# Attention and expert layer on one core: squares of the weights on ScalarE, two more weight pieces in the first loads, a third place for x, scales and splits earlier

## The chip, the core and the metric

The kernel runs on one core of a Trainium2 chip. The metric is the device time of one execution in microseconds (us), lower is better. A core has TensorE (PE, with its weight loads shown as PEld), VectorE (DVE), ScalarE (ACT), GpSimd (POOL) and SyncE (SP), whose queue issues every DMA of this kernel. Each engine works through its own list of instructions in the order of the built program, and waits on semaphores for the others.

## What is computed

The reference is a linear attention, whose output is the input of a feed-forward layer with a gate:

```python
q_s = np.exp(q - q.max(-1, keepdims=True));  q_s /= q_s.sum(-1, keepdims=True) + 1e-09
k_s = np.exp(k - k.max(2, keepdims=True));   k_s /= k_s.sum(2, keepdims=True) + 1e-09
kv = np.einsum('bhsd,bhse->bhde', k_s, v)            # batch 8, heads 8, seq 576, head_dim 64
x = np.einsum('bhsd,bhde->bhse', q_s, kv)            # then transposed to 4608 tokens x 512
h = x @ w_in                                          # 512 x 2048
g = h * erf(softplus(h))
out = g @ w_out                                       # 2048 x 512
```

All inputs are float32 here, except that the two weight matrices arrive as 64-bit numbers, which the kernel reads as pairs of 32-bit integers and turns into float32 itself.

## The kernel before

**Tiling.** The 4608 tokens are 12 blocks of 384 (`T`), three blocks for two batches. The 2048 columns of the hidden layer are four quarters. An item `n` is one block and one quarter, so there are 48; items 0 to 3 are block 0, items 4 to 7 block 1 and so on. An item has these steps, whose letters stand in the string `ORDER`: `m` is x times w_in (into `pX`, `pY`, `pZ`, from there to `H`), `T` softplus and `G` erf on ACT, `U` the product with h on DVE (L931), `I` and `O` the high and the low half of the result in float16 (L946 and L950), and `M` the product with w_out (into `o`).

**Two kinds of items.** Items 0 to 3 multiply in float32: `mm1_32` (L894) and the branch of `mm2` at L969. They need the weights only as float32. From item 4 on both products run in float16 with a high and a low half of each operand: seven products for four quarters of the matrices at L855, and three matmuls for one at L978. For them the weights are scaled and split (`wsplit`, `wsplit_sums`, letters `S` and `R`), and so is x (`finish`, steps `f`).

**Weights.** There are eight jobs, a quarter of w_in or of w_out each, in the order of `JOBS` (jobs 0, 1, 3 and 5 are w_in's, 2, 4, 6 and 7 w_out's), and each is loaded in two pieces of 1 MB (`wload`). A piece lands in one of several places (`raw`, or the tiles `wt` of jobs whose split is still far off); `wdecode` (letter `D`, L190, L194, L197) turns it into float32 with three DVE operations and, as it frees the place, asks for the next piece. `LOADS` is the order of the first loads: each `w` in it is one piece.

**Scales.** `wsquares` (`Q`) finds a bound of the squares of a job: 16 matmuls of 128x128 blocks with themselves (L224, tile `gram`) and a maximum on DVE (L225). `wscales` (`Z`, from L236) needs all eight, and gives the scales; no split can be done ahead of it.

**Attention.** The generator `attention(b)` hands out batch b in small shares; each `A` in `ORDER` takes one, and from item 4 on `pace` takes as many as a goal says, worked out from `n1`, `SHARES` and `LEAD`. Its matmuls for k and v are `kv_mm` (L503, tiles `kv_0` and `kv_1`), after which the loads of the next batch's k and v are issued (`load_kv`). x of a batch is written from PSUM by ACT (`x_put`, L405), times a scale `sx` for batches 0 and 1. `x_free` says when a block of x has a place; there are two.

**What sets the order.** The code is emitted as `ORDER` says, and then item by item; a scheduler of the framework then orders the instructions of each engine by what they depend on. `SPLITS` names the splits that are emitted in items 4 to 6. SP issues its DMAs in the order of its list: one that must wait holds up all that stand behind it.

Of the kernel before, what the change touches and what calls it, by code (L numbers as in the profile page):

```python
# [9 lines left out]
F32 = mybir.dt.float32  # L10
I32 = mybir.dt.int32
BF16 = mybir.dt.bfloat16
AF = mybir.ActivationFunctionType
# [9 lines left out]

CHAIN_FROM, CHAIN_TAIL = 2, 11

LOADS = "qkwwvwww"

# [4 lines left out]
    qm0 qm1 kmax kT kB qe0 qn0 ks2 ks0 D0.0 ks1 ke2 ke0 ke1 w6 kv0 kn0 D0.1 qe1 qn1 kv1 t0  # L34
    kn1 kvs x0 t1 lkv t2 x2 t3 x1 x3
    m0.0 D1.0 m0.1 D1.1 m0.2 m0.3 T0 G0 Q0
    D2.0 A m1.0 D2.1 m1.1 U0 m1.2 m1.3 T1 G1 Q1 A A D3.0 M0.0 D3.1 M0.1 M0.2 Q2 U1 A
    m2.0 D4.0 m2.1 D4.1 m2.2 m2.3 T2 G2 Q3 A A M1.0 D5.0 M1.1 D5.1 M1.2 U2 A A Q4
    m3.0 D6.0 m3.1 D6.1 m3.2 m3.3 T3 G3 A A A M2.0 D7.0 M2.1 D7.1 M2.2 U3 Q5 Q6 Q7 Z A A A A
    S0 R0 f0 f1 M3.0 M3.1 M3.2 S1 R1  # L40
"""

SPLITS = {4: "S2 S3 R3", 5: "S4 S5 R5", 6: "S6 S7"}

SHARES = [2.51, 0, 0.16, 0.09, 1.58, 2.43, 1.12, 0.26, 0.29, 0.04, 0.78, 1.12, 0.16]
LEAD = 2.0
# [7 lines left out]
def attn_moe_kernel(  # L54
# [158 lines left out]

    def wsquares(jn):

        which, g = wjobs[jn]
        o = 24 + 4 * (which == "out") + g
        bk = bank(f"gram_{jn}")  # L220
        top = stg[jn].bitcast(BF16).rearrange("p (n two) -> p n two", two=2)[:, :, 1]
        for i in range(16):
            blk = top[:, i * P:(i + 1) * P]
            nc.tensor.matmul(bk[:, :P], blk, blk, start=(i == 0), stop=(i == 15))  # L224
        nc.vector.tensor_reduce(small[:, o:o + 1], bk[:, :P], axis=AX.X, op=ALU.max)  # L225
        wsq.add(jn)

    def wscales():
# [99 lines left out]
    def x_free(i):  # L328


        return i < 2 or (("m", NG - 1, 3) in emitted if i == 2 else i - 2 in x7)

    def xblock(i):

        if i not in xbl:
            assert x_free(i)
            xbl[i] = xp.tile([P, NC4, T], F32, tag="xs", name=f"x_{i}")
        return xbl[i]

    x_next = [1]  # L340
# [60 lines left out]
    def bank(name):  # L401
        return psa.tile([P, 512], F32, tag="bk", name=name)
# [191 lines left out]
    def x_split(b, c, bk):  # L594
        for blk, off, o, w in xcols(b, 0 if b % 2 == 0 else SM + 2 * TAIL, SM):
            x_put(
                bk[:, o:o + w], xblock(blk)[:, c, off:off + w],
                bat[b]["sx"] if b < E32 else None,
            )

    def attention(b):
# [298 lines left out]
    def unit(b, g):  # L900

        U = bat[b]["U"][:, g:g + 1]
        if b < 2 and (b, g) not in udone:
            udone.add((b, g))
            nc.vector.tensor_tensor(U, w_u["in"][:, g:g + 1], bat[b]["ux"], op=ALU.mult)
        return U
# [3 lines left out]
    def flat(t):  # L910
        return t.rearrange("p f t -> p (f t)")
# [4 lines left out]
    def softplus(n):  # L916
        s, g = st[n], seq[n][2]
        s["G"] = ch.tile([P, FG, T], F32, tag="G", bufs=2, name=f"G_{n}")
        for o, w, b in spans(n):
            h, sp = s["H"], s["G"]  # L920
            h, sp = (flat(t) if w == T else t[:, :, o:o + w] for t in (h, sp))
            u = bat[0]["ux"] if n < NG else unit(b, g)
            act(sp, h, AF.Softplus, chain=in_chain(n), scale=u)

    def erf(n):
# [2 lines left out]

    def gmul(n):
        s, g = st[n], seq[n][2]  # L930
        nc.vector.scalar_tensor_tensor(  # L931
            flat(s["G"]), flat(s["G"]), bat[0]["ux"] if n < NG else GA[:, g:g + 1],
            flat(s["H"]), op0=ALU.mult, op1=ALU.mult,
        )
        if n < NG:
            return
        assert "all" in wready

        hl = flat(s["H"]).bitcast(F16)
        s["gh"], s["gl"] = (  # L940
            hl[:, i * GE:(i + 1) * GE].rearrange("p (f t) -> p f t", f=FG) for i in range(2)
        )
# [113 lines left out]
    w_even = sum(SHARES[:9]) + NC4 * sum(SHARES[11:])  # L1056
    w_odd = w_even + sum(SHARES[9:11])
    per_pair = w_even + w_odd
    n1 = NG + 1

    def pace(at_n):

# [67 lines left out]
```

## Time and profile before

| | us |
|---|---|
| median of 3 runs | 897.55 (896.29 to 899.88) |
| profiled execution, its time | 895.81 |
| its span, first to last instruction | 894.0 |
| PE busy | 841.5 (94% of the span) |
| DVE busy | 659.0 (74%) |
| ACT busy | 484.8 (54%) |

Busy time is the time in which at least one instruction of an engine ran; matmuls overlap, so their durations add up to more. The profiled execution took 895.81, of which 1.8 us lie outside the span. A line of the timeline shows the start, how long it took, the engine, the line of the kernel and the tiles; in brackets stands how long the engine had been idle and what ended that.

### The profile page before, as it was taken

What the parts mean: (1) busy time and instruction counts of PE and PEld (TensorE: products, weight loads), DVE (VectorE), ACT (ScalarE), POOL (GpSimd) and SP (SyncE); (2) the same over time, 40 slices, a digit from 0 to 9 for tenths busy, and PEclk for the clock granted to TensorE, in tenths of its full rate; (3) what the DMA queues carried; (4) which work ended last, traced back from release to release, by engine and by line L of the source; (5) the groups of instructions that cost most, each with busy time, mean ns of one, the idle gap of its engine ahead of it and who ended that gap; (6) DMA issues with size and microseconds to landing.
All of it is one profiled execution on the core that took longest, in us unless ns stands there. A gap on an engine that the chain in (4) does not pass through costs nothing.

```text
span 894.0 us, 15683 instructions
## 1 busy us (share of the span) xinstructions
PE 841.5 (94%) x6684; PEld 581.4 (65%) x6684; DVE 659.0 (74%) x908; ACT 484.8 (54%) x581; POOL 6.4 (1%) x14
## 2 busy tenths in 40 slices
PE   2899997688989999999999999999999999999997
PEld 1555554665766766766767767767767767676763
DVE  7889669999996687876896596877885575644453
ACT  2274156775673655654663655644754645553532
POOL 2000000000000000000000000000000000000000
PEclk9999998799999999999999999999999999999999
DMA  9864812401124120412033120311010000000100
GB/s 272 297 201 153 226 40 71 101 1 24 25 60 99 26 60 1 92 46 48 1 83 78 25 60 12 84 50 35 14 48 1 11 26 2 24 14 1 36 1 35
DMA packets 117381, 55.53 MB, mean 62 GB/s; under 512 B 106560, under 2 KB 108608, under 8 KB 117312
## 3 DMA queue, kind: packets, MB, share of 16 engines
q1 hardware_dynamic: 117312, 54.54, 22.2%
q8 instruction: 52, 0.85, 0.4%
q14 instruction: 17, 0.14, 0.0%
HBM read 45.09 MB, written 9.44 MB: 61 GB/s over the span
## 4 chain that ended last, share of the span: by engine, by line
PE 66%; DVE 21%; ACT 10%; issue 2%; DMA 1%; SPq 0%; ACTq 0%; DVEq 0%
PE o L978 27%; PE pX L855 14%; PE pZ L855 7%; ACT G L317 5%; ACT L317 4%; PE o L969 3%; PE pY L855 3%; DVE G L931 3%; DVE H L950 3%; PE kv L503 2%; PE pX L894 2%; DVE kmax L459 2%; DVE H L946 1%; DVE wt L270 1%; PE pY L894 1%
## 5 line engine op out<-in xcount | busy, mean ns | idle before, releaser
L978 PE MATMUL o<-wt,H 128*128 128x512 f16 x1584 | 366.7, 379 | 4.5 <-DVE H L950 3.2
L855 PEld LDWEIGHTS <-wt 128*128 128x128 f16 x3696 | 312.6, 99 | 47.8 <-issue 23.3
L978 PEld LDWEIGHTS <-H 128*128 128x128 f16 x1584 | 152.4, 98 | 158.8 <-DVE H L950 3.8
L855 PE MATMUL pX<-x,wt 128*128 128x192 f16 x2112 | 206.9, 248 | 6.5 <-DVE H L877 4.6
L317 ACT ACT_TABLE_LOAD x104 | 133.4, 1283 | 8.9 <-DVE H L880 7.1
L931 DVE SCALAR_TENSOR_TENSOR G<-G,small,H 128x1536 f32<-128x1536 f32 x44 | 80.0, 1817 | 69.0 <-ACT G L317 68.7
L855 PE MATMUL pZ<-x,wt 128*128 128x192 f16 x1056 | 104.6, 248 | 6.5 <-ACT x L269 4.7
L882 ACT COPY H<-pX 128x384 f32<-128x384 f32 x44 | 21.0, 477 | 148.8 <-PE pX L855 148.8
L317 ACT ACTIVATE G<-H,U 128x768 f32<-128x768 f32 (+1 forms) x60 | 72.8, 1231 | 22.1 <-DVE H L880 21.5
L950 DVE TENSOR_TENSOR H<-G,H 128x1536 f16<-128x1536 f32 x44 | 77.3, 1756 | 1.0
L317 ACT ACTIVATE G<-G 128x1536 f32<-128x1536 f32 x48 | 71.2, 1484 | 0.5
L855 PE MATMUL pY<-x,wt 128*128 128x192 f16 x528 | 52.3, 248 | 4.6 <-DVE H L867 4.6
L405 ACT ACTIVATE x<-x 128x384 f32<-128x384 f32 (+1 forms) x48 | 15.9, 378 | 56.5 <-PE x L590 54.8
L867 DVE COPY H<-pY 128x384 f32<-128x384 f32 x44 | 24.3, 552 | 30.0 <-PE pY L855 30.0
L946 DVE CAST H<-G 128x1536 f16<-128x1536 f32 x44 | 42.0, 956 | 0.8
L994 DVE TENSOR_SCALAR ob<-o,V 128x512 f32<-128x512 f32 x29 | 21.7, 747 | 25.4 <-PE o L978 25.3
L270 DVE SCALAR_TENSOR_TENSOR x<-x,x 128x768 f16<-128x768 f32 (+1 forms) x44 | 37.2, 848 | 4.2 <-ACT x L269 4.1
L269 ACT ACTIVATE x<-x 128x768 f16<-128x768 f32 (+1 forms) x44 | 33.0, 761 | 12.7 <-DVE x L361 12.7
L880 DVE TENSOR_TENSOR H<-pZ,H 128x384 f32<-128x384 f32 x44 | 24.2, 550 | 19.0 <-PE pZ L855 19.0
L869 DVE TENSOR_TENSOR H<-pX,H 128x384 f32<-128x384 f32 x44 | 24.3, 553 | 14.7 <-PE pX L855 14.5
L361 DVE TENSOR_TENSOR x<-x 128x384 f32<-128x384 f32 x44 | 24.2, 551 | 7.0 <-ACT x L405 6.7
L877 DVE TENSOR_TENSOR H<-pX,H 128x384 f32<-128x384 f32 x44 | 24.2, 549 | 5.1 <-PE pX L855 5.0
(158 smaller groups left out, 811.8 us busy)
## 6 DMA issues: line engine op xcount, KB each, us to landing
out_dram<-ob SPq DMA_DIRECT2D x32, 256.0 KB, 2.3
vbuf<-in_v_dram SPq DMA_DIRECT2D x60, 128.0 KB, 3.1
wt<-in_moe_w_out_dram SPq DMA_DIRECT2D x7, 1024.0 KB, 8.7
q<-in_q_dram SPq DMA_DIRECT2D x56, 128.0 KB, 2.9
k<-in_k_dram SPq DMA_DIRECT2D x56, 128.0 KB, 3.1
wt<-in_moe_w_in_dram SPq DMA_DIRECT2D x5, 1024.0 KB, 8.9
raw<-in_moe_w_in_dram SPq DMA_DIRECT2D x3, 1024.0 KB, 6.8
H_raw<-in_k_dram SPq DMA_DIRECT2D x2, 512.0 KB, 6.6
```

Source lines behind the costliest of these rows:

```text
L269: nc.scalar.activation(hi, src, AF.Copy, scale=s)
L270: nc.vector.scalar_tensor_tensor(lo, src, s, hi, op0=ALU.mult, op1=ALU.subtract)
L317: i = nc.scalar.activation(out_, in_, func, **kw)
L855: nc.tensor.matmul(o, w[wl][:, c, a * P:(a + 1) * P], x[:, xl, xi, c, :], start=(new and a == 0 and c == 0 and i == 0), stop=(c == 1 and i ...
L867: nc.vector.tensor_copy(C[0, 0], bank2("Y"))
L869: add(C[0, 0], bank2("X"), C[0, 0], op=ALU.add)
L894: nc.tensor.matmul(ph[:, :T], w[:, c, a * P:(a + 1) * P], x[:, c, :], start=(c == 0), stop=(c == NC4 - 1),)
L931: nc.vector.scalar_tensor_tensor(flat(s["G"]), flat(s["G"]), bat[0]["ux"] if n < NG else GA[:, g:g + 1], flat(s["H"]), op0=ALU.mult, op1=A ...
L946: nc.vector.tensor_copy(flat(s["gh"]), flat(s["G"]))
L950: nc.vector.tensor_tensor(flat(s["gl"]), flat(s["G"]), flat(s["gh"]), op=ALU.subtract)
L969: nc.tensor.matmul(o, s["G"][:, a, ts_], w[:, a, :], start=(first_ and a == 0), stop=(last_ and a == FG - 1),)
L978: nc.tensor.matmul(o, s[gt][:, a, ts_], w[wl][:, a, :], start=(first_ and a == 0 and i == 0), stop=(last_ and a == FG - 1 and i == 2),)
```

## The change

- `wsquares` leaves the matmuls away: four ACT operations `Square` over 128x512 each, with a sum along the row (`accum_out`), and a maximum of the four sums on DVE. PE has no part in it any more. What ACT writes besides the sums goes to a PSUM bank and is not read.
- `LOADS` has two more `w`: the first loads are seven pieces and not five. The two pieces that used to be asked for by the first two decodes are now issued at the start; the first two decodes ask for the next two.
- x has three places (`bufs=3`), and `x_free` follows.
- Block 0's x is stored without a scale; softplus of items 0 to 3 has a scale of 1, and their product `U` is a plain product of two tensors.
- In `ORDER` some decodes and shares of the attention are moved; `Z`, `S0` and `R0` stand ahead of `M2` now and not behind it, `S1`, `R1` ahead of `M3` and `S2` right behind it. `SPLITS` has the rest, earlier by one or two. `n1` is larger by two, which lets `pace` begin later and then go faster.

```diff
-LOADS = "qkwwvwww"
+LOADS = "qkwwvwwwww"
...
-    D2.0 A m1.0 D2.1 m1.1 U0 m1.2 m1.3 T1 G1 Q1 A A D3.0 M0.0 D3.1 M0.1 M0.2 Q2 U1 A
-    m2.0 D4.0 m2.1 D4.1 m2.2 m2.3 T2 G2 Q3 A A M1.0 D5.0 M1.1 D5.1 M1.2 U2 A A Q4
-    m3.0 D6.0 m3.1 D6.1 m3.2 m3.3 T3 G3 A A A M2.0 D7.0 M2.1 D7.1 M2.2 U3 Q5 Q6 Q7 Z A A A A
-    S0 R0 f0 f1 M3.0 M3.1 M3.2 S1 R1
+    D2.0 A m1.0 D2.1 m1.1 U0 m1.2 m1.3 T1 G1 Q1 A A D3.0 M0.0 D3.1 M0.1 M0.2 Q2 U1 A A
+    m2.0 D4.0 m2.1 D4.1 m2.2 m2.3 T2 G2 Q3 A A D5.0 M1.0 D5.1 M1.1 M1.2 U2 A A Q4 D6.0
+    m3.0 D6.1 m3.1 D7.0 m3.2 D7.1 m3.3 T3 G3 Q5 Q6 Q7 Z A A S0 A A R0 M2.0 A A M2.1 A A M2.2
+    A A f0 f1 U3 S1 R1 M3.0 M3.1 M3.2 S2
...
-SPLITS = {4: "S2 S3 R3", 5: "S4 S5 R5", 6: "S6 S7"}
+SPLITS = {4: "S3 R3 S4", 5: "S5 R5 S6", 6: "S7"}
...
-        bk = bank(f"gram_{jn}")
-        top = stg[jn].bitcast(BF16).rearrange("p (n two) -> p n two", two=2)[:, :, 1]
-        for i in range(16):
-            blk = top[:, i * P:(i + 1) * P]
-            nc.tensor.matmul(bk[:, :P], blk, blk, start=(i == 0), stop=(i == 15))
-        nc.vector.tensor_reduce(small[:, o:o + 1], bk[:, :P], axis=AX.X, op=ALU.max)
+        m = at.tile([P, 4], F32, tag="sq", name=f"sq_{jn}")
+        for i in range(4):
+            nc.scalar.activation(
+                bank(f"sq_{jn}_{i}"), stg[jn][:, i * 512:(i + 1) * 512], AF.Square,
+                accum_out=m[:, i:i + 1],
+            )
+        nc.vector.tensor_reduce(small[:, o:o + 1], m, axis=AX.X, op=ALU.max)
...
-        return i < 2 or (("m", NG - 1, 3) in emitted if i == 2 else i - 2 in x7)
+        return i < 3 or (("m", NG - 1, 3) in emitted if i == 3 else i - 3 in x7)
...
-            xbl[i] = xp.tile([P, NC4, T], F32, tag="xs", name=f"x_{i}")
+            xbl[i] = xp.tile([P, NC4, T], F32, tag="xs", bufs=3, name=f"x_{i}")
...
-                bat[b]["sx"] if b < E32 else None,
+                1.0 if blk == 0 else bat[b]["sx"] if b < E32 else None,
...
-            u = bat[0]["ux"] if n < NG else unit(b, g)
+            u = 1.0 if n < NG else unit(b, g)
...
+        if n < NG:
+            nc.vector.tensor_tensor(flat(s["G"]), flat(s["G"]), flat(s["H"]), op=ALU.mult)
+            return
...
-    n1 = NG + 1
+    n1 = NG + 3
```

Three places of the built program show how instructions move. The first is PE, item 1's product with w_out (`o_0`, `o_1`, `o_2`) and around it; `kv_0` and `kv_1` are the matmuls of k and v of batch 1, and `pX_0` begins item 3. Before:

```order
L969 MATMUL o_0_468<-wt_99,G_426 128x512 x4
L969 MATMUL o_1_478<-wt_99,G_426 128x512 x4
L969 MATMUL o_2_483<-wt_99,G_426 128x512 x4
L503 MATMUL kv_1_630<-vbuf,k_1_291 64x65 x8
L503 MATMUL kv_1_630<-vtail,kt_109 64x65 x2
L503 MATMUL kv_1_630<-vbuf,k_1_291 64x65 x8
L503 MATMUL kv_1_630<-vtail,kt_109 64x65 x2
L894 MATMUL pX_0_708<-x_134,wt_100 128x384 x4
```

After:

```order
L969 MATMUL o_0_452<-wt_99,G_418 128x512 x4
L969 MATMUL o_1_462<-wt_99,G_418 128x512 x3
L502 MATMUL kv_1_576<-vbuf,k_1_294 64x65
L969 MATMUL o_1_462<-wt_99,G_418 128x512
L502 MATMUL kv_1_576<-vbuf,k_1_294 64x65 x7
L502 MATMUL kv_1_576<-vtail,kt_109 64x65 x2
L502 MATMUL kv_1_576<-vbuf,k_1_294 64x65
L969 MATMUL o_2_467<-wt_99,G_418 128x512
L502 MATMUL kv_1_576<-vbuf,k_1_294 64x65 x7
L502 MATMUL kv_1_576<-vtail,kt_109 64x65 x2
L969 MATMUL o_2_467<-wt_99,G_418 128x512 x3
L893 MATMUL pX_0_683<-x_136,wt_100 128x384 x3
```

The matmuls of `kv_1` end with three of the four products of `o_2` still to come, where all twelve stood ahead of them before.

The second is SP's list. `raw`, `wt_93` and `wt_94` are the three places through which the last weight pieces come, `k_0`, `k_1`, `kt`, `vbuf` and `vtail` the loads of k and v (the first `vbuf` for batch 1, the others for batch 2); the load of `k_1` waits until the matmuls of `kv_1` have read the batch before. Before:

```order
L174 DMA wt_94<-in_moe_w_out_dram 128x2x1024
L381 DMA vbuf<-in_v_dram 128x4x64 x4
L174 DMA raw_615<-in_moe_w_out_dram 128x2x1024
L174 DMA wt_93<-in_moe_w_out_dram 128x2x1024
L381 DMA k_0_656<-in_k_dram 128x4x64 x4
L381 DMA k_1_661<-in_k_dram 128x4x64 x4
L395 DMA kt_666<-in_k_dram 64x8x64 x2
L381 DMA vbuf<-in_v_dram 128x4x64 x4
L395 DMA vtail<-in_v_dram 64x8x64
L174 DMA wt_94<-in_moe_w_out_dram 128x2x1024
```

After:

```order
L174 DMA wt_94<-in_moe_w_out_dram 128x2x1024
L380 DMA vbuf<-in_v_dram 128x4x64 x4
L380 DMA k_0_602<-in_k_dram 128x4x64 x4
L380 DMA k_1_607<-in_k_dram 128x4x64 x4
L394 DMA kt_612<-in_k_dram 64x8x64 x2
L380 DMA vbuf<-in_v_dram 128x4x64 x4
L394 DMA vtail<-in_v_dram 64x8x64
L174 DMA raw_626<-in_moe_w_out_dram 128x2x1024
L174 DMA wt_93<-in_moe_w_out_dram 128x2x1024
L174 DMA wt_94<-in_moe_w_out_dram 128x2x1024
```

The second piece of job 6 (`raw`) and the first of job 7 (`wt_93`) stood ahead of the loads of k and now stand behind them; the last piece (`wt_94`) is where it was.

The third is DVE between the last pieces and the scales. `sg_714` and `sg_778` (after: `sg_677` and `sg_698`) are the float32 weights of jobs 6 and 7, `wse_in` the first operation of the scales behind the transposes on PE. Before:

```order
L225 TENSOR_REDUCE small<-gram_689 128x1
L190 TENSOR_SCALAR sg_778<-wt_94 128x1024
L194 SCALAR_TENSOR_TENSOR sg_778<-wt_94,sg_778 128x1024
L197 SCALAR_TENSOR_TENSOR sg_778<-wt_94,sg_778 128x1024
L931 SCALAR_TENSOR_TENSOR G_740<-G_740,x_u,H_707 128x1536
L270 SCALAR_TENSOR_TENSOR x_1_947<-x_135,x_1_947 128x768
L416 TENSOR_REDUCE qt_m<-qt_760 128x8
L417 TENSOR_TENSOR qt_760<-qt_760,qt_m 128x512
L225 TENSOR_REDUCE small<-gram_794 128x1
L225 TENSOR_REDUCE small<-gram_812 128x1
L225 TENSOR_REDUCE small<-gram_830 128x1
L240 TENSOR_REDUCE wse_in<-ws_in 128x4
```

After:

```order
L194 SCALAR_TENSOR_TENSOR sg_677<-raw_626,sg_677 128x1024
L197 SCALAR_TENSOR_TENSOR sg_677<-raw_626,sg_677 128x1024
L190 TENSOR_SCALAR sg_698<-wt_93 128x1024
L931 TENSOR_TENSOR G_717<-G_717,H_682 128x1536
L194 SCALAR_TENSOR_TENSOR sg_698<-wt_93,sg_698 128x1024
L190 TENSOR_SCALAR sg_698<-wt_94 128x1024
L197 SCALAR_TENSOR_TENSOR sg_698<-wt_93,sg_698 128x1024
L194 SCALAR_TENSOR_TENSOR sg_698<-wt_94,sg_698 128x1024
L224 TENSOR_REDUCE small<-sq_730 128x1
L197 SCALAR_TENSOR_TENSOR sg_698<-wt_94,sg_698 128x1024
L224 TENSOR_REDUCE small<-sq_740 128x1
L239 TENSOR_REDUCE wse_in<-ws_in 128x4
```

Between the last decode (its third row is the last L197) and `wse_in` now stands one small maximum; item 3's product (L931), one row of x's split, two on the next batch's `qt` and three maxima stood there before. Three decodes stand in a row now, the first of them begun one row ahead of these, and item 3's product is among them.

## Rows read from the trace of the kernel before

**Rows 1.** The profile's page: span, and busy time of each engine.

```profile
span 894.0 us, 15683 instructions
PE 841.5 (94%) x6684; PEld 581.4 (65%) x6684; DVE 659.0 (74%) x908; ACT 484.8 (54%) x581; POOL 6.4 (1%) x14
```

**Rows 2.** Busy time of each engine by stretch; the first row names columns.

```profile
core 0: us, PE busy (x) PEld busy (x) DVE busy (x) ACT busy (x) POOL busy (x), PEclk, DMA share, GB/s
39.40:126.93 87.53, 86.55 (x425) 50.05 (x424) 70.89 (x91) 40.74 (x47) 0.95 (x1) 1.00 0.57 167
...
142.50:222.15 79.65, 61.07 (x520) 46.07 (x519) 74.94 (x101) 52.12 (x61) 0.00 (x0) 0.87 0.17 41
222.15:328.60 106.45, 102.99 (x897) 73.65 (x896) 86.47 (x120) 59.61 (x76) 0.00 (x0) 1.00 0.23 56
328.60:894.00 565.40, 554.99 (x4655) 390.24 (x4652) 379.82 (x509) 308.66 (x362) 0.00 (x0) 1.00 0.13 33
```

**Rows 3.** Groups by line: PE's matmuls for the squares (busy, mean ns).

```profile
L224 PE MATMUL gram<-wt 128*128 128x128 bf16 x96 | 6.5, 218 | 0.0
L224 PE MATMUL gram<-sg 128*128 128x128 bf16 x32 | 2.0, 218 | 0.0
```

**Rows 4.** Timeline of DVE from the last piece to the scales, and later.

```profile
113.30 0.69 DVE L190 TENSOR_SCALAR sg<-wt 128x1024 int32<-128x1024 int32 x1 [7.61 <-DMA wt<-in_moe_w_out_dram]
115.29 1.24 DVE L197 SCALAR_TENSOR_TENSOR sg<-wt,sg 128x1024 int32<-128x1024 int32 x1
117.88 1.82 DVE L931 SCALAR_TENSOR_TENSOR G<-G,x_u,H 128x1536 f32<-128x1536 f32 x1 [1.36 <-ACT G L317]
...
124.66 0.29 DVE L225 TENSOR_REDUCE small<-gram 128x1 f32<-128x128 f32 x1 [2.70 <-PE gram L224]
...
126.93 0.69 DVE L240 TENSOR_REDUCE wse_in<-ws_in 128x4 f32<-128x512 f32 x1
...
152.14 0.54 DVE L867 COPY H<-pY 128x384 f32<-128x384 f32 x1
```

**Rows 5.** Timeline of SP's queue: loads of batch 2's k, and the last piece.

```profile
90.64 11.61 SPq L381 DMA_DIRECT2D k<-in_k_dram  x8
...
107.14 1.51 SPq L174 DMA_DIRECT2D wt<-in_moe_w_out_dram  x1
```

**Rows 6.** Timeline of PE: item 1's product, `kv_1`, first float16 product, items 6 and 12.

```profile
87.20 10.57 PE L969 MATMUL o<-wt,G 128*128 128x512 f32 x24
...
99.19 0.33 PE L503 MATMUL kv<-vtail,kt 64*64 64x65 f32 x4
...
142.92 1.15 PE L855 MATMUL pY<-x,wt 128*128 128x192 f16 x12
...
221.42 0.81 PE L978 MATMUL o<-wt,H 128*128 128x512 f16 x3
...
328.60 1.67 PE L978 MATMUL o<-wt,H 128*128 128x512 f16 x7
```

**Rows 7.** Groups of ACT, shapes apart: rows of 512 and of 1536 elements.

```profile
L317 ACT ACTIVATE G<-G 128x1536 f32<-128x1536 f32 x48 | 71.2, 1484 | 0.5
...
L317 ACT ACTIVATE qt<-qt 128x512 f32<-128x512 f32 x4 | 2.5, 617 | 3.3 <-DVE qt L417 3.3
```

**Rows 8.** Groups of DVE: operations of the attention and of x's split.

```profile
L270 DVE SCALAR_TENSOR_TENSOR x<-x,x 128x768 f16<-128x768 f32 (+1 forms) x44 | 37.2, 848 | 4.2 <-ACT x L269 4.1
L429 DVE TENSOR_TENSOR q<-q,q_r 128x1024 f32<-128x1024 f32 x16 | 19.5, 1218 | 0.1
L572 DVE TENSOR_TENSOR qTs<-qT,qTs 128x512 f16<-128x512 f32 x24 | 16.4, 684 | 6.0 <-ACT qTs L571 6.0
L557 DVE SCALAR_TENSOR_TENSOR kvbd<-kvf,x_s,kvbd 64x256 f16<-64x256 f32 x12 | 5.8, 480 | 0.3
L556 DVE TENSOR_SCALAR kvbd<-kvf,x_s 64x256 f16<-64x256 f32 x12 | 4.2, 347 | 0.2
```

**Rows 9.** Group of PE: the attention's products that make x.

```profile
L590 PE MATMUL x<-qTs,kvbd 128*128 128x512 f16 x72 | 20.7, 379 | 2.9 <-DVE kvbd L556 1.6 <-ACT qTs L571 0.7 <-DVE qTs L572 0.5
```

More of the change, by code (lines that the diff above doesn't have):

```diff
@@ L930, in gmul @@
         s, g = st[n], seq[n][2]
+        if n < NG:
+            nc.vector.tensor_tensor(flat(s["G"]), flat(s["G"]), flat(s["H"]), op=ALU.mult)
+            return
         nc.vector.scalar_tensor_tensor(
-            flat(s["G"]), flat(s["G"]), bat[0]["ux"] if n < NG else GA[:, g:g + 1],
-            flat(s["H"]), op0=ALU.mult, op1=ALU.mult,
-        )
-        if n < NG:
-            return
+            flat(s["G"]), flat(s["G"]), GA[:, g:g + 1], flat(s["H"]),
+            op0=ALU.mult, op1=ALU.mult,
+        )
         assert "all" in wready
```

## The prediction

> **What bounds the kernel now.** The page comes first: PE is busy for 841.5 of 894.0 us and DVE for 659.0 [rows 1]. That is an average over stages with different limits, so the table by stretches comes next [rows 2]. In the float32 stage (39.4 to 126.93) PE is full, 86.55 of 87.53, and DVE is not, 70.89. From 142.5 to 222.15 it is the other way round: DVE works 74.94 of 79.65 us and PE 61.07, at a granted clock of 0.87. From 222.15 on PE is nearly full again: 102.99 of 106.45, then 554.99 of 565.4. So there are three limits in turn: PE, then DVE, then PE. What the middle one is worth shows in the lag: PE ends item 4's first float16 product at 144.1 [rows 6], and DVE copies it at 152.14 [rows 4], 8.1 us later. DVE is late because it idled before: 16.6 us in the float32 stage [rows 2], of which 7.61 in one wait for the last weight piece, and 2.70 in one wait for the matmuls of the squares [rows 4]. All scales begin at 126.93 [rows 4]; no split comes before. So I ask three things: when the scales begin, how much DVE has to do from there to item 6, and what PE has left from there.
>
> **Squares on ACT.** PE loses 128 matmuls. Their mean of 218 ns would make 27.9 us, but they overlap: the busy time of the two groups is 6.5 + 2.0 = 8.5 us, 1.06 a job [rows 3]. ACT gets 32 operations of 512 elements, at the row of ACT of that width 0.62 each [rows 7], so 20 us; beside ACT's 40.74 of 87.53 in the float32 stage [rows 2] there is room. No row shows one with a sum along the row: the lower bound is 0.62, the upper 1.48, ACT's row of three times the width; I take 0.62, whose width it is. On the path stand the last two squares of the last job, 1.2 us (up to 3.0), and five squares that the order of the change puts ahead of batch 1's exponentials of k, which have slack, since PE comes to `kv_0` only after item 2's products.
>
> **The last pieces and the scales.** In SP's list the last three pieces stand behind the loads of batch 2's k, which wait for `kv_1`. Before, `kv_1` ended at 99.5 [rows 6]. Four groups of matmuls for squares ahead of it go, 4.2 us [rows 3], and it moves ahead of three of item 1's twelve products: 10.57 / 12 x 3 = 2.6 us [rows 6]. That makes 92.7. SP took from 99.5 to 107.14 for the loads in between, 7.6 us [rows 5, 6], and the piece was there at 113.30, 6.2 us after its issue [rows 4]: the first of the three is now there at 92.7 + 7.6 + 6.2 = 106.5. DVE decodes three pieces in a row, each 0.69 + 1.24 + 1.24 (the middle operation taken like the last) = 3.2 [rows 4], together 9.5, and item 3's product among them, 1.8 [rows 4]: 117.8. The other two pieces are issued right behind and land while the first is decoded; if each needed its own 6.2 us, the end would be at 92.7 + 7.6 + 18.6 + 3.2 = 122.1. Behind the last decode come two squares and a transpose on PE, for which I take 2.0: the scales begin at 119.8 and not at 126.93. **That is -7.1**; with dearer squares, later pieces and PE's queue between 0 and -10. The two more pieces at the start cost nothing on the path: SP issues them while it would wait for PE's transposes, and the loads of batch 1 that land later by them are hidden by the decodes that they make possible, which DVE now does first; without that cover they would cost up to 2 x 6.2 us. Their gain, decodes without a wait, is in the sum above: DVE comes to the last three pieces early, and must wait there for the same loads that held up one piece before. So most of DVE's idle time stays, and that is why the gain is not 16.6.
>
> **DVE from the scales to item 6.** The instructions of DVE between `wse_in` and item 6's low half are the same, except that attention of batch 2 has moved behind: one operation like L429, two like L572, two like L557, two like L556, so 1.2 + 1.4 + 1.0 + 0.7 = 4.3 us [rows 8], and some tiny ones that I leave out. One of x's split has come in, 0.8 [rows 8]. **That is -3.5.** DVE's idle time in this stretch, 79.65 - 74.94 = 4.7 [rows 2], I leave as it is; it may vanish (-4.7) or double. The unscaled x of block 0 saves next to nothing: ACT stores the rest of the same product with the scale a few rows further, and waits there for the same scale; the plain products of items 0 to 3 stay one pass of DVE. The third place for x lets batch 1's x be written sooner; the splits that used it are in the sum.
>
> **PE from item 6 on.** Item 6 begins its second product at 221.42, item 12 at 328.60 [rows 6]; from there the lists of both engines are the same. Between them PE gets what was put off, six products that make x, 20.7 / 72 x 6 = +1.7 us [rows 9]. It idled 3.5 us there [rows 2]; with DVE less late I take the later share, 10.4 of 565.4, so 2.0: -1.5. **Together +0.2**, bounds -1.8 and +2.
>
> **Sum.** -7.1 - 3.5 + 0.2 = -10.4 us. The profiled execution took 895.81, so 885.4. The median of the runs is 897.55, 1.7 above it, so 887. With the bounds of the terms it is 882 to 892.
>
> **Rivals.**
>
> *DVE catches up.* The float32 stage ends 8.5 us sooner, and if the pieces come in time and DVE's 4.7 us of idle time go as well, the gain is 10.4 + 4.7 + some 2 = 17: 880. For it speaks that no DVE wait in the middle stretch is long; against it that ACT, at 52.12 of 79.65 there [rows 2], gets its work in less time.
>
> *Only PE's work counts.* If PE is the limit throughout, the gain is the squares' 8.5 us [rows 3]: 889. For it speaks PE's 94% [rows 1], against it DVE's 74.94 of 79.65 in the middle [rows 2]. The Trainium skill, Perfetto Trace Analysis, section Identifying the Most-Contended Engine, tells to improve the engine of highest occupancy first, which is PE and gives this result; the stretches show that here another engine sets the end for 80 us, which the same page allows for kernels whose limit changes over time.
>
> *The queue eats it.* If `kv_1` is not sooner, since the order of the decodes ahead of item 1's product or the squares ahead of the exponentials hold it up, three pieces come behind it where one did: decodes end at 113.3 + 9.5 + 1.8 = 124.6, the scales begin at 126.6, and only the 3.2 us of the later terms are left: 894. With `kv_1` 2 us later than before it is 896, no change.
>
> *The clock.* PE has less to do ahead of the splits, and waits longer for item 4's halves. In the middle stretch a granted 0.87 means (1 - 0.87) x 2 x 79.65 = 21 us at 1.2 GHz [rows 2], at most 10 of them lost: PE's work there is at least 51 us at full clock, 49 without the products put off. Were the clock at 1.2 GHz throughout, it would take 98 us from the end of the float32 stage, 142.5 - 8.5 = 134: item 6 would begin its second product at 232, 10.6 later than before, and the time would be 908. Slower by 4.5 us it is from 85 us at 1.2 GHz; 21 were seen, so this is unlikely. The Trainium skill, TensorE: Matmul & The Clock Gate, Part 1, says that PE falls to half its rate when it has idled and comes back after sustained work; this trace agrees as far as its clock is below 1.00 in the one stretch where PE idles most.
>
> **How the numbers follow.** 0.5% is 4.5 us, about what a measurement of this kernel can tell from no change. The forecast has a chance of 0.50 (887, own range 882 to 892), DVE catching up 0.16 (880), PE alone 0.13 (889), the queue 0.14 (894 to 898, so no change), the clock 0.07 (908). Faster by over 0.5%, below 893.1: 0.50 + 0.16 + 0.13 = 0.79; the same 0.14; slower 0.07. The range of 8 in 10 leaves out the clock and the far ends of the first rival and of the queue: 879 to 897.
>
> **What would show it.** In the profile of the changed kernel `wse_in` should begin near 120, with one wait of DVE of 5 to 12 us for a DMA that ends near 106; `kv_1` should end near 93; DVE should be full from there to item 6, whose low half should end near 211; item 12 should begin its second product near 318, and the rest of the span should be 565 us as before. I am wrong if the wait for the pieces is gone or much longer, if a square takes over 1 us, if PE and not DVE is full between 135 and 210, or if PE idles more after item 12.

## The result, and the profile of the changed kernel

| | before | changed |
|---|---|---|
| median, us | 896.9 (896.29 to 899.88) | 888.34 (886.76 to 891.66) |
| ratio, 95% interval | | 0.9902, 0.9874 to 0.9929 |
| profiled execution, us (span) | 895.81 (894.0) | 886.76 (884.9) |
| predicted, us | | 887 (879 to 897) |

The change gains 8.6 us, 1%. The time was forecast within 1.4 us, and faster was the likeliest case. Both medians are of five runs here; the 897.55 that the forecast started from is that of the first three. The kernel before had medians of 896.8 to 898.1 in the comparisons below, each on one chip; so the measure there is the ratio to the kernel before run beside on the same chip: 0.001 is 0.9 us.

The page of the changed kernel, its span and busy times, against [rows 1]:

```profile
span 884.9 us, 15492 instructions
PE 832.7 (94%) x6556; PEld 573.0 (65%) x6556; DVE 656.9 (74%) x908; ACT 504.5 (57%) x645; POOL 6.4 (1%) x14
```

PE has 8.8 us less to do (the two groups of [rows 3] were 8.5), ACT 19.7 more, and there are 64 instructions more on ACT, since each square has a second one that reads its sum. The busy times by stretch, against [rows 2]. The borders are the scales (120.82) and the end of the low half of items 6 and 12; the first row names the columns:

```profile
core 0: us, PE busy (x) PEld busy (x) DVE busy (x) ACT busy (x) POOL busy (x), PEclk, DMA share, GB/s
39.40:120.82 81.42, 80.89 (x299) 42.82 (x298) 67.20 (x89) 56.16 (x100) 0.00 (x0) 1.00 0.58 159
120.82:142.00 21.18, 18.27 (x100) 11.31 (x99) 20.68 (x52) 17.43 (x28) 1.90 (x2) 1.00 0.38 100
142.00:209.24 67.24, 53.76 (x471) 39.95 (x470) 65.81 (x81) 47.58 (x51) 0.00 (x0) 0.90 0.15 34
209.24:312.12 102.88, 97.33 (x845) 69.48 (x846) 84.34 (x129) 60.61 (x78) 0.00 (x0) 1.00 0.22 53
319.60:884.90 565.30, 554.43 (x4656) 390.29 (x4653) 379.96 (x509) 308.59 (x362) 0.00 (x0) 1.00 0.13 33
```

The same three limits follow each other: PE is full until the scales, DVE from there to item 6 (65.81 of 67.24, where it was 74.94 of 79.65), PE behind. The last row is the one of before, 565.3 for 565.4: all of the gain comes ahead of item 12.

DVE from the first wait to the low half of item 6, as a timeline, against [rows 4]; the middle rows of each decode are left out:

```profile
99.78 0.16 DVE L224 TENSOR_REDUCE small<-sq 128x1 f32<-128x4 f32 x1 [1.25 <-ACT sq L220]
102.97 0.16 DVE L224 TENSOR_REDUCE small<-sq 128x1 f32<-128x4 f32 x1 [3.04 <-ACT sq L220]
105.74 0.69 DVE L190 TENSOR_SCALAR sg<-raw 128x1024 int32<-128x1024 int32 x1 [2.61 <-DMA raw<-in_moe_w_out_dram]
...
111.96 1.76 DVE L931 TENSOR_TENSOR G<-G,H 128x1536 f32<-128x1536 f32 x1 [2.29 <-ACT G L316]
...
117.77 1.23 DVE L197 SCALAR_TENSOR_TENSOR sg<-wt,sg 128x1024 int32<-128x1024 int32 x1
120.45 0.16 DVE L224 TENSOR_REDUCE small<-sq 128x1 f32<-128x4 f32 x1 [1.46 <-ACT sq L220]
120.82 0.69 DVE L239 TENSOR_REDUCE wse_in<-ws_in 128x4 f32<-128x512 f32 x1 [0.21 <-PE ws_in L235]
...
207.49 1.75 DVE L950 TENSOR_TENSOR H<-G,H 128x1536 f16<-128x1536 f32 x1
```

The wait for the weight piece (7.61 before) is there as 2.61, with 3.04 and 1.25 ahead of it for squares; together it is 6.9 us until 105.74, so the engine still stands still until the same loads come. The queue that they come through, on SP, against [rows 5]:

```profile
84.35 10.95 SPq L380 DMA_DIRECT2D k<-in_k_dram  x8
...
100.19 0.57 SPq L174 DMA_DIRECT2D raw<-in_moe_w_out_dram  x1
100.86 0.93 SPq L174 DMA_DIRECT2D wt<-in_moe_w_out_dram  x2
```

And PE, the end of `kv_1` and the first float16 product, against [rows 6]:

```profile
92.29 0.33 PE L502 MATMUL kv<-vtail,kt 64*64 64x65 f32 x4
...
133.27 1.15 PE L854 MATMUL pY<-x,wt 128*128 128x192 f16 x12
```

The three pieces are issued from 100.19 on, 7.6 us behind the end of `kv_1` at 92.6.

### The profile page after: what moved, and what is told of

The parts are those of the page before. It is cut to its first block, busy times and chain, and to the rows that moved or that the text cites. A ratio compares the mean times of both kernels' runs of the same rounds, so it can differ in the third digit from the quotient of the medians.

```text
span 884.9 us, 15492 instructions
## 1 busy us (share of the span) xinstructions
PE 832.7 (94%) x6556; PEld 573.0 (65%) x6556; DVE 656.9 (74%) x908; ACT 504.5 (57%) x645; POOL 6.4 (1%) x14
## 4 chain that ended last, share of the span: by engine, by line
PE 65%; DVE 20%; ACT 10%; issue 3%; DMA 1%; SPq 1%; ACTq 0%; DVEq 0%
PE o L978 26%; PE pX L854 14%; PE pZ L854 7%; ACT G L316 5%; ACT L316 4%; PE o L969 3%; PE pY L854 3%; DVE G L933 3%; PE kv L502 3%; PE pX L893 2%; DVE H L950 2%; DVE kmax L458 2%; DVE wt L269 2%; PE qT L577 1%; PE pY L893 1%
## 5 line engine op out<-in xcount | busy, mean ns | idle before, releaser
L316 ACT ACTIVATE G<-H,U 128x768 f32<-128x768 f32 (+1 forms) x60 | 73.0, 1232 | 22.7 <-DVE H L879 22.1
L404 ACT ACTIVATE x<-x 128x384 f32<-128x384 f32 (+1 forms) x52 | 17.7, 386 | 55.0 <-PE x L589 52.8
L868 DVE TENSOR_TENSOR H<-pX,H 128x384 f32<-128x384 f32 x44 | 24.4, 555 | 14.4 <-PE pX L854 14.2
L458 DVE TENSOR_REDUCE kmax<-k 128x256 f32<-128x1024 f32 x14 | 27.6, 1980 | 0.0
```

What stands on the lines that cost most here:

```text
L316: i = nc.scalar.activation(out_, in_, func, **kw)
L458: nc.vector.tensor_reduce(kmax[:, hf * 4:hf * 4 + 4, :], ks[hf], axis=AX.X, op=ALU.max)
```

## The experiments

Theory A is the prediction's: the scales' time and DVE's work from there to item 6 set the middle of the kernel. Theory B is the rival that only PE's work counts; with 889 it gave nearly the measured time, so the total can't tell the two apart. All times are medians.

| kernel | us | ratio to before, 95% | scales begin | low half ends, item 4 / 6 / 12 |
|---|---|---|---|---|
| before | 896.9 | 1 | 126.93 | 182.9 / 222.1 / 321.0 |
| changed | 888.3 | 0.9902 (0.9874 to 0.9929) | 120.82 | 172.4 / 209.2 / 312.1 |
| sq_only | 892.5 | 0.9947 (0.9928 to 0.9965) | 123.41 | 179.0 / 217.8 / 320.0 |
| sq_pe | 890.6 | 0.9908 (0.9873 to 0.9944) | 117.17 | 174.6 / 213.0 / 317.6 |
| m3_cut | 892.7 | 0.9942 (0.9919 to 0.9966) | 121.31 | 167.6 / 212.2 / 317.3 |
| dve_cut | 882.9 | 0.9836 (0.9817 to 0.9855) | 120.82 | 172.1 / 203.8 / 308.1 |
| old_loads | 891.6 | 0.9929 (0.9906 to 0.9952) | 122.46 | 175.1 / 213.4 / 316.3 |
| n1_old | 889.9 | 0.9907 (0.9879 to 0.9935) | 120.61 | 179.0 / 217.7 / 314.5 |
| x_scaled | 888.7 | 0.9899 (0.9869 to 0.9929) | 120.96 | 174.3 / 211.0 / 316.0 |
| order_old | 884.4 | 0.9858 (0.9835 to 0.9881) | 120.73 | 169.7 / 208.2 / 309.6 |
| before_kv | 898.1 | 1.0002 (0.9986 to 1.0017) | 126.98 | 183.1 / 222.4 / 322.9 |
| kv_behind | 877.6 | 0.9771 (0.9749 to 0.9793) | 111.47 | 162.3 / 205.3 / 303.1 |
| kv_sq_first | 881.2 | 0.9815 (0.9787 to 0.9844) | 107.94 | 163.8 / 200.6 / 305.4 |
| kv_n1_more | 874.1 | 0.9734 (0.9716 to 0.9753) | 111.52 | 160.7 / 190.2 / 297.7 |

The last two columns come from each kernel's one profiled execution. Executions of one kernel spread over 2 to 7 us, so a trace shows the place of a loss better than its size: the changed kernel's is of its fastest run, those of sq_only, sq_pe and x_scaled are of their slowest, and x_scaled, whose time is the changed kernel's, ends item 12's low half 3.8 us later.

### Is it PE's work or DVE's?

**sq_pe**, the squares as matmuls again, in the changed kernel: the body of `wsquares` is that of the kernel before.

> The changed kernel with one part undone: the squares are matmuls on PE again. Theory A: PE's float32 stage ends 8.5 us later, near 142, but DVE is late by as much there anyway; kv_1 ends near 97, two pieces stand behind the loads of k in place of three, the scales come at 120 to 123 and item 6's second product at 208 to 211: 0 to 3 us slower than the changed kernel, 888 to 891. Theory B: PE has 8.5 us more to do and the time is 897.

Measured: 0.9908 for 0.9902, no difference that the intervals show; by the medians 2.2 us. Giving PE its 8.5 us back costs a quarter of that by the medians. That is theory A's size, not B's. One thing to read with care there: `wse_in` at 117.17 covers w_in alone; the last square came at 120.64, the scales of w_out at 122.31.

**m3_cut**, less PE work, nine of item 3's twelve products with w_out left out:

```diff
-            for a in range(FG):
+            for a in range(3 if n == 3 else 0, FG):
                 nc.tensor.matmul(
                     o, s["G"][:, a, ts_], w[:, a, :],
```

> The changed kernel without nine of the twelve float32 products of item 3 with w_out (their part of the output is left out), so PE has 9/12 of 10.5 = 7.9 us less to do ahead of the float16 items and everything else stays. Theory A: DVE is the limit from 133 to 207, PE only waits longer there, and may lose some to a lower clock: 0 to 1.5 us faster than the changed kernel, 887 to 888. Theory B: 7.9 us faster, 880.5.

Measured: 892.7, 3.6 us above the changed kernel by the ratios (the intervals overlap by 0.0010), its five runs (891.35 to 893.4) above the median of the other. B, with 880.5, is out; A's gain of 0 to 1.5 did not come either. The busy times by stretch, first of the changed kernel, then of m3_cut (columns as above):

```profile
120.00:140.00 20.00, 19.09 (x105) 11.95 (x104) 18.84 (x50) 16.72 (x30) 1.90 (x2) 1.00 0.38 101
140.00:160.00 20.00, 10.68 (x100) 9.46 (x100) 20.00 (x25) 14.11 (x15) 0.00 (x0) 0.83 0.03 6
160.00:180.00 20.00, 14.98 (x110) 11.37 (x108) 19.91 (x22) 16.45 (x19) 0.00 (x0) 0.83 0.00 1
180.00:200.00 20.00, 19.27 (x195) 12.94 (x194) 20.00 (x27) 12.90 (x13) 0.00 (x0) 1.00 0.37 83
```

```profile
120.00:140.00 20.00, 15.20 (x94) 9.94 (x94) 18.42 (x53) 18.15 (x32) 1.90 (x2) 1.00 0.39 105
140.00:160.00 20.00, 13.25 (x120) 12.00 (x120) 19.33 (x20) 15.26 (x17) 0.00 (x0) 0.81 0.01 3
160.00:180.00 20.00, 16.69 (x104) 10.85 (x104) 18.84 (x19) 13.25 (x15) 0.00 (x0) 0.77 0.00 1
180.00:200.00 20.00, 14.85 (x145) 9.53 (x144) 20.00 (x30) 11.78 (x12) 0.00 (x0) 0.83 0.24 54
```

With less work PE idles 4.8 us from 120 to 140 where it idled 0.9, and its granted clock is lower in the three rows behind: (1 - clock) x 2 x 20 gives 24 us at 1.2 GHz for 14. DVE has two gaps that it did not have (19.33 and 18.84): from the scales to item 6's low half its work is the same (86.61 us for 86.49) and its idle time 2.4 us more, in waits for PE's products and for erf. The scheduler also ordered DVE's list anew, and item 5's low half slipped by 2.3 us although item 4's came 4.8 sooner. How much of the 4 us is the clock and how much the order was not separated. The mean clock of a run does not sort the times: three runs of m3_cut had 0.981 to 0.984 and took 891.35 to 893.4, two of the changed kernel had 0.976 and 0.977 and took 888.65 and 888.34.

**dve_cut**, less DVE work, eight additions and subtractions of weight blocks left out:

```diff
-        for o, x, y, op in (
+        for o, x, y, op in () if jn > 1 else (
             ((1, 1), (1, 0), (1, 1), ALU.add), ((1, 0), (0, 0), (1, 0), ALU.subtract),
```

> The changed kernel without the eight additions and subtractions of weight blocks of jobs 3 and 5 on DVE (two of the four quarters of w_in are then combined wrongly, so that output is not the reference's). That is 8 x 0.60 = 4.8 us of DVE's work between the scales and item 6; PE, ACT and the loads have the same work as before. Theory A (DVE sets the time from 133 to 207): item 6's low half ends 3 to 5 us sooner than 209.2, and after what is paid back behind it the time is 2 to 4.8 us below the changed kernel, 883.5 to 886. Theory B (only PE's work counts): 888, within 1 us.

Measured: 0.9836, 5.9 us below the changed kernel by the ratios, 3.8 by the spans of the two traces. Item 6's low half ends 5.5 sooner. So 4.8 us less on DVE move the end by 4 to 6, and 7.9 us less on PE do not move it forward: the middle is DVE's. The Trainium skill, Perfetto Trace Analysis, section Identifying the Most-Contended Engine, would have us improve the engine of highest occupancy first. By the matmuls that is PE with 94%, and these two runs say the contrary for the 67 us from 142 to 209. But the same section does not judge TensorE by its matmuls' busy share; one of the two measures that it names instead is that of the weight loads, 65% here, which is below DVE's 74%. So the prediction's reading of that section, PE by its 94%, left out half of it. Its section Optimization Strategy, which looks for gaps within the stretch of one regime, fits these runs.

### What each part of the change is worth

**sq_only**, the kernel before with `wsquares` of the changed one and no other edit:

> The kernel before with one part of the change alone: the squares on ScalarE. Theory A (the time of the scales and DVE's work from there to item 6 set the middle of the kernel): kv_1 ends 4.2 us sooner, near 95.3, and the last piece and the scales (126.93 before) come sooner by at least as much; DVE's work behind the scales stays, so 3.5 us of the whole change's gain are missing, and the 2.6 us of item 1's products too: about 4 us gained, 893. If DVE's waits for the matmuls of the squares (2.70 and less) go as well, the scales come near 117 and the gain is up to 8. Theory B (only PE's work counts): the 8.5 us of the matmuls, all of the gain of the whole change, 888.

Measured: 892.5, ratio 0.9947, 4.8 us gained; theory A said about 4, and B's 888 lies outside the interval. `kv_1` ends at 97.07, 2.5 us sooner and not 4.2. The scales come 3.5 sooner only, though no matmul is in their way any more. DVE of this kernel, item 3's product and the scales:

```profile
114.54 1.82 DVE L930 SCALAR_TENSOR_TENSOR G<-G,x_u,H 128x1536 f32<-128x1536 f32 x1 [9.00 <-ACT G L316]
...
123.41 0.69 DVE L239 TENSOR_REDUCE wse_in<-ws_in 128x4 f32<-128x512 f32 x1 [0.65 <-PE ws_in L235]
```

The wait has changed its place: 9.00 us for item 3's erf on ACT, with the last decode behind it in DVE's list.

**old_loads**, one edit, `LOADS = "qkwwvwww"` in the changed kernel:

> The changed kernel with five weight pieces at the start in place of seven. The prediction said that the two pieces cost nothing and give DVE decodes without a wait, while the last three pieces wait for kv_1 in either case. If that holds, DVE idles earlier (60 to 85) and kv_1 and the last pieces come at the same time within 1 us, scales at 120.8 to 122: 0 to 1.5 us slower, 888 to 890. If the decodes of jobs 3 to 5 come so late that the float32 products wait on PE, kv_1 and all behind it shift by the wait, 3 us or more: above 891.

Measured: 0.9929, 2.4 us above the changed kernel by the ratios, though their intervals overlap. The scales are 1.6 later, because `kv_1` is (94.3 for 92.6) and the whole stage with it: from 60 to 80 PE is busy for 19.14 of 20.00 us, where it is full in the changed kernel, with one wait of 0.9 for DVE's maximum of k. So the place of kv_1 was not the same within 1 us, and the two pieces are worth those 1.6 us at the scales, which the sum had no term for.

**n1_old**, `n1 = NG + 1` in the changed kernel:

> The changed kernel with the old n1, so that the shares of attention of batch 2 are spread as before and 4.3 us of DVE's operations come back ahead of item 6. By the prediction's own terms item 6's low half ends 3.5 us later than in the changed kernel (209.2), near 213, and six products of PE (1.7 us) lie ahead of it again; if that is a net gain of the change, the time is 1.5 to 3.5 us above the changed kernel, 890 to 892. The other theory: PE is nearly full from item 6 on and what is put off ahead of item 6 is paid back behind it (between the second products of items 6 and 12 the changed kernel took 112.0 us, the kernel before 107.2): then item 6 is later but item 12 is not, and the time is 888, within 1 us.

Measured: 0.9907 for 0.9902, no difference shown; 1.5 us by the medians. The trace shows both theories at work. Item 6's low half ends 8.5 us later (217.7 for 209.2), more than the 4.3 us that I had counted as moved, and then from item 6 to item 12 it takes 96.8 for 102.9. Of 8.5 us put off, 6.1 are paid back.

**x_scaled**, the factor `sx` and `ux` restored for block 0:

> The changed kernel with block 0's x scaled again, and softplus and the products of items 0 to 3 with its factor. The prediction said that this part saves next to nothing, since one pass of DVE stays one pass and ACT waits for the same scale a few rows on: within 1 us of the changed kernel, 887.5 to 889.5. The rival: the first x block waits for the chain of the scale (maximum, transpose, exponent) ahead of the float32 products, so that PE's first item begins 1 to 3 us later and all behind it: 889.5 to 891.

Measured: 0.9899, the changed kernel's ratio. As predicted, this part is worth nothing that can be measured. The third place for x was not undone alone. The trace shows one thing more. `kv_1` ends at 90.12 here, 2.5 us sooner than in the changed kernel, and the first of the last pieces is decoded 1.25 us sooner; the scales still begin at 120.96, since DVE waits longer for item 3's erf:

```profile
104.49 0.69 DVE L190 TENSOR_SCALAR sg<-raw 128x1024 int32<-128x1024 int32 x1 [2.73 <-DMA raw<-in_moe_w_out_dram]
...
112.99 1.82 DVE L930 SCALAR_TENSOR_TENSOR G<-G,x_u,H 128x1536 f32<-128x1536 f32 x1 [3.25 <-ACT G L316]
```

So in the changed kernel two conditions lie close together ahead of the scales, the pieces and that erf.

**order_old**, the old `ORDER` and `SPLITS` in the changed kernel:

> The changed kernel with the old ORDER and the old SPLITS, everything else kept. Theory A by the terms of the prediction: kv_1 moves behind item 1's products again, 2.6 us later (95.2), in SP's list only one piece stands behind the loads of k, the scales begin 1 to 3 us later than 120.8, and the splits lose their earlier place: 1.5 to 4 us slower than the changed kernel, 890 to 892. Theory B: PE's work is the same, 888.

Measured: 884.4, ratio 0.9858: about 4 us faster than the changed kernel (the intervals overlap by 0.0007). So this part of the change looks like a loss, and I had it as a gain. Scales at 120.73, as in the changed kernel, although `kv_1` ends at 94.3: one piece stands behind it in place of three, and what holds up DVE is item 3's erf:

```profile
111.54 1.76 DVE L931 TENSOR_TENSOR G<-G,H 128x1536 f32<-128x1536 f32 x1 [8.80 <-ACT G L316]
...
120.73 0.69 DVE L239 TENSOR_REDUCE wse_in<-ws_in 128x4 f32<-128x512 f32 x1 [0.97 <-PE ws_in L235]
```

Then DVE needs 49.0 us to item 4's low half, and 51.6 in the changed kernel. Taken by line and shape, the groups of DVE in that stretch and their counts are the same in both, with one exception, which only the changed kernel has:

```profile
L269 DVE SCALAR_TENSOR_TENSOR wt<-sg,small,wt 128x2048 f16<-128x2048 f32 x1 | 2.3, 2347 | 0.0
```

It is the low half of the split of job 6. Its first use is item 6's second product, 40 us later; the old `SPLITS` had `S6` in item 6, the new one in item 5, and the scheduler put it ahead of item 4's halves. On an engine without idle time that delays item 4 by its whole 2.35 us. "Sooner" for one is later for another. It accounts for item 4, 2.7 us; with the old order item 6's low half is only 1.0 sooner and item 12's 2.5, so the rest of the 4 us has no cause shown.

Undone one at a time, the parts cost 0.5 us (squares), 2.4 (loads), 0.4 (`n1`), -0.3 (x's scale) and -3.9 (order) by the ratios, together less than nothing of a gain of 8.8, and none is clear of the intervals. So the parts do not add up: the squares alone gain 4.8 on the kernel before, and undoing them in the changed one loses next to nothing. The stretches show where the gain lies; how it is shared among the parts, the third place for x among them, stays open.

### The queue

**kv_behind**, the changed kernel with batch 2's k and v issued behind the last piece (`L` stands behind `D6.0` in `ORDER`):

```diff
+        if c == "L":
+            assert nxt[0] == NPC * NJ
+            with tc.issue_after(lastw[0]):
+                load_kv(2)
```

> The changed kernel with the loads of batch 2's k and v issued behind the last three weight pieces, not ahead of them. Theory A (the pieces hold up the scales, through SP's queue): the three pieces are issued as their places come free, from 88 to 95, none is waited for at 105, the scales begin at 112 to 116 in place of 120.8, DVE gets 5 to 8 us ahead, item 6's second product comes 3 to 8 us sooner and some of it is given back to PE behind: 1.5 to 6 us faster than the changed kernel, 882 to 887. Theory B: nothing changes for PE, 888. A third possibility: k of batch 2 comes too late for attention and holds up DVE or PE behind item 6, slower than 890.

Measured: 877.6, ratio 0.9771, 11.8 us below the changed kernel by the ratios. The last pieces on SP, and DVE from the end of the decodes on:

```profile
84.37 1.93 SPq L175 DMA_DIRECT2D raw<-in_moe_w_out_dram  x1
87.97 8.69 SPq L175 DMA_DIRECT2D wt<-in_moe_w_out_dram  x2
96.71 6.72 SPq L381 DMA_DIRECT2D k<-in_k_dram  x8
```

```profile
104.64 1.20 DVE L198 SCALAR_TENSOR_TENSOR sg<-wt,sg 128x1024 int32<-128x1024 int32 x1
110.50 0.16 DVE L225 TENSOR_REDUCE small<-sq 128x1 f32<-128x4 f32 x1 [4.66 <-ACT sq L221]
111.47 0.69 DVE L240 TENSOR_REDUCE wse_in<-ws_in 128x4 f32<-128x512 f32 x1 [0.81 <-PE ws_in L236]
...
113.78 1.75 DVE L932 TENSOR_TENSOR G<-G,H 128x1536 f32<-128x1536 f32 x1
```

The first of the three pieces is issued 15.8 us sooner, no decode waits, the last ends at 105.84 and not at 119.0, and the scales are 9.35 us sooner. Not all of that is the pieces: item 3's product, whose erf held DVE up ahead of the scales in the changed kernel, stands behind them now (113.78). Item 4's low half is 10.1 us sooner, item 6's only 3.9, item 12's 9.0: DVE does 4.7 us more ahead of item 6 (91.15 for 86.49 from the scales on), and PE has 3.2 less between items 6 and 12 (94.11 for 97.33). So the gain of the scales' time arrives almost whole at item 12, as theory A had it, but not through item 6 alone; its size was taken too small in the expectation, since I had allowed for more to be paid back behind item 6.

**before_kv**, the same edit in the kernel before:

> The kernel before with one edit: the loads of batch 2's k and v are issued behind the last weight piece. There one piece stood behind them, waited for 7.61 us until 113.30. Theory A: the last piece is decoded as soon as DVE has time, by 108 to 112 in place of 116.5, but the matmuls of the last squares still stand behind float32 products on PE, so that the scales come 2 to 5 us sooner than 126.93 and the time is 2 to 5 us below the kernel before, 892 to 895. The rival: the squares on PE set the time of the scales alone, and nothing is gained: 896 to 898.

Measured: 1.0002, no gain at all. DVE of this kernel:

```profile
106.30 1.22 DVE L198 SCALAR_TENSOR_TENSOR sg<-wt,sg 128x1024 int32<-128x1024 int32 x1
...
117.92 1.82 DVE L932 SCALAR_TENSOR_TENSOR G<-G,x_u,H 128x1536 f32<-128x1536 f32 x1 [10.15 <-ACT G L318]
124.70 0.29 DVE L226 TENSOR_REDUCE small<-gram 128x1 f32<-128x128 f32 x1 [2.70 <-PE gram L225]
...
126.98 0.69 DVE L241 TENSOR_REDUCE wse_in<-ws_in 128x4 f32<-128x512 f32 x1
```

The decodes are done at 107.5, where the kernel before ended them at 116.5, and the scales still begin at 127: the squares stand in PE's list behind float32 products, and their matmuls end when they did. The rival of this run's expectation was right. At least two conditions end together at the scales, the pieces through SP and the squares through PE; item 3's erf, for which DVE waits 10.15 us here, is close to them. Moving the loads alone gains 0, the squares alone 3.5 at the scales, both together, with the rest of the change, 15.5; both without the rest were not run.

**kv_sq_first**, kv_behind with `Q5 Q6 Q7` ahead of `T3 G3` in `ORDER`:

> The kernel with the loads of batch 2 behind the last weight pieces (877.6), and besides with the last squares ahead of item 3's softplus and erf in the order. There DVE waited 4.66 us for the last square, which stood behind a table load and the softplus on ACT, 2.7 us. Theory A: the scales begin 2.7 us sooner, at 108.8, and DVE, which has no idle time from there to item 6, passes it on: 1.5 to 3 us faster, 874.5 to 876. The rival: item 3's erf comes 2 us later, its float32 product and PE behind it wait, or the other order of the instructions costs as much: 877 to 879.

Measured: 881.2, ratio 0.9815, 3.9 us above kv_behind by the ratios (the intervals overlap by 0.0006), with the scales 3.5 us sooner. Item 4's low half ends at 163.8 for 162.3: the same split of job 6 (2.33 us here) has come ahead of it, which it is not in kv_behind, and DVE idles 2.8 us in between where it had no gap. But that is not where the time goes: item 6's low half ends 4.7 us sooner than in kv_behind, and item 12's 2.3 later, 104.8 us for 97.8 between them, with 99.19 us of PE's work there for 94.11. The other order of the instructions, the rival, fits; which of them cost it stays open.

**kv_n1_more**, kv_behind with `n1 = NG + 5`:

> The version with the loads of batch 2 behind the last pieces (877.6), with n1 larger by another two, which puts still more of batch 2's attention behind the splits. If DVE's work ahead of item 6 still sets the time there and is not paid back: 874 to 876.5. If it is paid back behind item 6, where PE is nearly full: 877 to 879. If x of batch 2 comes too late for its items: above 880.

Measured: 874.1, ratio 0.9734, the fastest: 22.7 us below the kernel before, run beside it, 3.3 below kv_behind by the ratios (the intervals overlap by 0.0004). Item 6's low half ends 15.1 us sooner than in kv_behind, item 12's 5.4: again about two thirds are paid back, and what is left is a gain.

## Why the prediction was right, point by point

- **kv_1 and the pieces.** `kv_1` was to end at 92.7 and ended at 92.62; the first of the last pieces was to be decoded from 106.5 on, and was at 105.74. The wait of 5 to 12 us came as three waits of 6.9 us together. The number came out better than its terms, 4.2 us for the squares and 2.6 for three products passed. Undone in the changed kernel, the squares are worth 4.0 (`kv_1` at 96.63), the order 1.7 (94.30), and the two more pieces, which the working had at nothing on the path, 1.6 (94.25); on the kernel before, the squares alone gave 2.5. With the old order the scales do not move: the order that brought `kv_1` forward also put two more pieces behind it.
- **Decodes and scales.** 117.8 was forecast for the end of the decodes, 119.0 came; DVE waited 2.29 us for item 3's erf, which the working had not as a wait; it holds DVE up longer where DVE comes to it sooner (3.25 in x_scaled, 8.80 in order_old). Scales at 119.8 forecast, 120.82 came: -6.1 for -7.1.
- **The squares.** 0.62 us each: 0.60 and a read of the sum of 0.19, most of it under the next square, one each 0.61 to 0.63. The last two took the 1.5 us of the wait at 120.45. The slack that I gave to squares ahead of the exponentials was there. Not foreseen: the PSUM bank that a square writes to has to come free first.
- **DVE from the scales to item 6's low half.** Forecast -3.5 with the idle time unchanged, bounds to -4.7 more; came -6.8 (95.2 to 88.4). DVE's work there fell by 3.9 us, which is the term, and its idle time by 2.9, from 4.8 to 1.9. The likeliest value of the idle time was wrong, its bound right: that much of the rival that DVE catches up came true. The low half was to end near 211 and ended at 209.2.
- **PE from item 6 on.** Forecast +0.2; came +4.0 from one low half to the other (98.9 to 102.9). PE's work rose by 1.6 us, as forecast (1.7), but its idle time by 2.4, where I had taken 1.5 off. That is the step that failed: I took "DVE less late" as less idle time on PE, but the work put off comes to DVE too, behind item 6: 84.34 us for 78.9 in the kernel before. With the old `n1` it is 76.55, and PE idles 3.0 us there for 5.6.
- **Sum.** -6.1 - 6.8 + 4.0 - 0.2 = -9.1 for -10.4. The errors of the two middle terms, 3.3 and 3.8 us, have opposite signs, so the sum is better than its terms: that part of its closeness is luck. The forecast's own range, 882 to 892, is also narrower than what the stated bounds add up to, some 878 to 901.
- **What was not seen.** That the reordering looks like a loss of about 4 us inside the gain. I read `SPLITS` as bringing splits "in the sum" without asking what stands behind them on a full engine.
- **The rivals.** That only PE's work counts gave 889 and would have passed for right on the time alone; m3_cut, dve_cut and sq_pe refute it. The queue: three pieces behind `kv_1` do cost, up to 9.35 us at the scales, as kv_behind shows, but on top of a gain and not in its place. The clock: 0.90 for 0.87 in the middle, no loss here; the one trace of m3_cut has a lower clock there, with less for PE to do ahead of the stretch.

## What to carry to other kernels

Ask in each stretch which engine has no gaps: work ahead of the first use on that engine is not free, however early it is ready (2.35 us here), and work put off from it is a gain only as far as the next stretch has room, about a third of it here. Where two chains end at one point, cutting one alone brings little or nothing (the loads 0 us, the squares 3.5 of 15.5 at the scales); look for the other before you call a cause harmless. Parts that are undone one at a time need not add up to the whole. An order that is changed in one place moves instructions in others, so look at the list before you name a cause. And when a time agrees with a rival too, take work from each engine in turn to see whose it is.

## What the runs showed of the hardware

A square with a sum along its row is two instructions on ACT, here the first ones of a stretch that waited for a bank of PSUM and then for the chain of x's scale:

```profile
95.30 0.60 ACT L220 ACTIVATE sq<-wt 128x512 f32<-128x512 f32 x1 [8.90 <-DVE kvbd L531]
...
97.80 0.60 ACT L220 ACTIVATE sq<-wt 128x512 f32<-128x512 f32 x1 [1.78 <-DVE x_e L122]
98.33 0.19 ACT L220 ACTIVATION_READ_ACCUMULATOR sq<-wt 128x1 f32 x1
98.43 0.58 ACT L220 ACTIVATE sq<-wt 128x512 f32<-128x512 f32 x1
```

From 97.80 to 98.43 it is 0.63 for one, 20 us for all 32. Its plain output, which nobody reads, goes to one of two banks that it shares with `kv_1`, and the first square waited 8.90 us, until DVE had read `kv_1` (L531); that was no loss here, since the pieces came later.

Less work on PE did not make the kernel faster: without 7.9 us of float32 products the granted clock from 140 to 200 was 0.81, 0.77 and 0.83 in the trace of m3_cut, in place of 0.83, 0.83 and 1.00, and the time rose by about 4 us; that the clock is the cause isn't shown. The Trainium skill, TensorE: Matmul & The Clock Gate, Part 1, says that PE falls to half its rate when it has idled. The rows agree in part: the 4.8 us of idle time up to 140, for 0.9, are followed by 0.81 for 0.83, but the lower 0.77 from 160 to 180 follows a stretch in which PE idled less (6.75 us for 9.32).
